# Attention with zero-padded k and v in SBUF, q stored unit by unit, transposes of 64 queries, and one MLP piece earlier

## The chip, the cores and the metric

The kernel runs on one core of one Trainium2 chip. The core has five engines that each work through their own instructions in order: TensorE (PE, with its weight loads shown apart as PEld), VectorE (DVE), ScalarE (ACT), GpSimd (POOL) and SyncE (SP), which here only issues DMA transfers. Engines wait for each other, and for transfers, through semaphores. The metric is the device time of one execution in microseconds (us); the kernel before takes 677.34 us, the median of three runs.

## The reference

Three layers follow each other. The first is attention with q, k, v of shape (2, 8, 576, 64): a pooled part and a local part, which are added.

```python
q_d = q.reshape(B, H, Sd, factor, D).mean(axis=3)      # factor = 4; k_d and v_d alike
out_d = sm_attn(q_d, k_d, v_d)                         # softmax attention over 144 pooled tokens
out_up = np.repeat(out_d, factor, axis=2)
mask = np.abs(pos[:, None] - pos[None, :]) < factor    # a query sees 3 keys on either side
scores = np.where(mask, scale * q @ k.T, -1e9)
...
return (out_up + softmax(scores) @ v).astype(np.float32)
```

Its output, 1152 tokens of 512 features, goes through `h = x @ w_in; g = h * clip(h + 3, 0, 6) / 6; g @ w_out` (hidden size 2048), and then through four weighted experts, `out += p[:, e] * (relu(x @ w1[e]) @ w2[e])` (hidden size 1024).

## The kernel before

**Units.** The attention works on eight units of two heads each, four for each of the two batches. For a unit, k and q stand with the 128 features of its two heads on the partitions and the 576 tokens along a row, and v stands with tokens on the partitions. Two units make a pair and share one k slot and one q slot; `load_qk` loads a pair (the first pair unit by unit), `load_v` loads a third of a batch's v.

**Local part.** The 576 queries are cut into 18 blocks of 32 (`WINDOWS`); a block sees 38 keys. `window(n)` gives the first of these keys, and at the two ends of the sequence it is moved inwards, so that the first and the last block have their queries elsewhere within their 38 keys than the other sixteen. The mask and the pooling weights `fours` therefore come in three kinds. `place(n)` sets a block's place: column group `j` (32 queries) and place `i`, whose parity `r = i % 2` says whether its keys stand on partitions 0 to 37 or 64 to 101 of a v slot. For this the v slots are loaded in runs of 112 rows (`WR2`: 48 rows from 0 on, and the next 64 from 64 on), which hold two blocks.

**Steps of a unit.** `sums` adds up k and q by fours on POOL (DVE for the first two units' k); `pooled_scores`, `masks`, `scores` are PE; `less_max`, `pooled_softmax`, `normalise`, `pooled_normalise` are DVE, ACT and POOL, where the last step is two POOL multiplications (`exd` by `recd`, `ex` by `rec`). `turn` transposes the 128 x 320 probabilities of each head on PE (`L610`) and copies them to `aT` on ACT; `pooled_turn` does so for the pooled part (`L678`). `values` multiplies by v (36 small products on `L698`, four pooled ones on `L709`) and adds both parts on DVE (`xf`).

**Order.** All engines follow the order in which the code is written during the attention. The loop over `t` interleaves the units: at turn `t` PE does `pooled_scores(t)`, `masks(t)`, `scores(t)`, `turn(t-1)`, `values(t-2)`, `pooled_turn(t-1)`; `idle_products` adds four 128 x 512 bf16 products of zeros ahead of `pooled_scores` and of `turn`, whose results are not used. POOL does the two multiplications of unit `t`, then `sums(t+2)`. SP issues transfers in the written order; up to eight are in flight, and the ninth waits for the first: pair 0, v of batch 0, pair 1, pair 2, the first weight block of the next layer (`w_in`), v of batch 1, and, written at the end of turn 1, pair 3. The last two turns (`t = 8, 9`) have no scores left; there `pieces(1)` puts single products of the next layer (`first`, 12 matrix products of 384 columns) between the steps. `convert` splits the next layer's weights into two parts on DVE and ACT, a step at a time.

Of the kernel before, what the change touches and what calls it, by code (L numbers as in the profile page):

```python
# [17 lines left out]
F32 = mybir.dt.float32  # L18
# [7 lines left out]
ALU = mybir.AluOpType  # L26
# [3 lines left out]
P = 128  # L30
# [9 lines left out]

QB = 32
# [8 lines left out]
WR2 = 112  # L50
# [8 lines left out]
NQ = 2 * QT + 2 * QB  # L59
# [53 lines left out]
def model(ctx: ExitStack, tc: tile.TileContext, qT, kT, v, dp, w_in, w_out, w1, w2, out):  # L113
# [246 lines left out]
    def load_qk(pair, units=(0, 1)):  # L360

        b, hp = divmod(2 * pair + units[0], NHP)
        if pair not in k_slots:
            k_slots[pair], q_slots[pair] = take(), take()
        n = len(units)
        at = units[0]
        nc.sync.dma_start(
            out=k_slots[pair][0][:, at * S : (at + n) * S].rearrange("p (u s) -> p u s", u=n),
            in_=kT[b, :, hp : hp + n],
        )  # L370
        q = q_slots[pair][0][:, : 2 * S].rearrange("p (s u c) -> p s u c", s=2, u=2)
        for s in range(2):
            nc.sync.dma_start(out=q[:, s, at : at + n], in_=qT[b, s, :, hp : hp + n, :])

    def window(n):
        return min(max(n * QB - (FACTOR - 1), 0), S - W)

# [10 lines left out]
    def load_v(b, p):  # L388
        v_slots.setdefault(b, []).append(take())
        if p < 2:  # L390
            if p == 0:
                v_rows(b, p, 0, window(0), WR, 0, 1)
                v_rows(b, p, WP, window(2), WR, 0, 1)
                v_rows(b, p, 0, window(1), WR2, 1, 2)
            else:
                v_rows(b, p, 0, window(8), WR2, 0, 2)
            v_rows(b, p, 0, window(8 * p + 4), WR2, 2, 4)
        else:
            v_rows(b, p, 0, window(16), WR, 0, 1)
            v_rows(b, p, 0, window(17), QB, 1, 2)  # L400
            v_rows(b, p, QB, window(17) + QB, W - QB, 1, 2)
# [8 lines left out]
    def pool_v(b):  # L410

        pool = banks(True)
        for m in range(4):
            for g in range(3):
                for r in range(2):
                    few = min(QB, KR[r] - g * QB)
                    if m * QB // FACTOR >= few:
                        continue
                    a, one = divmod(4 * g + m, 2)
                    n = 4 * a + 2 * r + one  # L420
                    i, j = place(n)
                    kind = 1 if n == 0 else 2 if n == NWIN - 1 else 0
                    rows = slice(r * WP, r * WP + W)
                    at = (3 - m) * QB // FACTOR
                    nc.tensor.matmul(
                        pool[g * QB : g * QB + few, r, :],
                        fours[rows, kind, at : at + few],
                        v_slots[b][i // 2][0][rows, j * DM : (j + 1) * DM],
                        start=(m == 0),
                        stop=((m + 1) * QB // FACTOR == few),  # L430
                    )
# [37 lines left out]
    def far(part, o):  # L469
        for sign in (1, -1):  # L470
# [4 lines left out]
                base=FACTOR - 1 + sign * o,  # L475
# [5 lines left out]
    far(mask[0:QB, 1:NI], FACTOR - 1)  # L481
    for j in range(1, NJ):
        nc.vector.tensor_copy(mask[j * QB : (j + 1) * QB, : NI - 1], mask[0:QB, 1:NI])
    far(mask[0:QB, 0:1], 0)
    far(mask[QB : 2 * QB, NI - 1 :], W - QB)
# [4 lines left out]
    fours = const.tile([P, 3, 7 * QB // FACTOR], F32, name="fours")  # L490

    def make_fours():
        nc.gpsimd.memset(fours[:WP], 0.0)
        own = slice(3 * QB // FACTOR, 4 * QB // FACTOR)
        nc.gpsimd.memset(fours[:WP, :, own], 1.0)
        for n, o in enumerate((FACTOR - 1, 0, W - QB)):
            for sign, at in ((1, -o), (-1, FACTOR - 1 + o)):
                nc.gpsimd.affine_select(
                    out=fours[:WP, n, own],
                    in_=fours[:WP, n, own],  # L500
                    pattern=[[-sign * FACTOR, QB // FACTOR]],
                    base=at,
                    channel_multiplier=sign,
                    compare_op=ALU.is_ge,
                    fill=0.0,
                )
# [6 lines left out]
    class Unit:  # L513
# [4 lines left out]
        def sums(self):  # L518
# [3 lines left out]
            self.k = k[:, o * S : (o + 1) * S]  # L522
            self.q = q[:, : 2 * S].rearrange("p (s u c) -> p s u c", s=2, u=2)[:, :, o]
            self.kd = k[:, 2 * S + o * PK : 2 * S + (o + 1) * PK]
            self.qd = q[:, 2 * S + o * PK : 2 * S + (o + 1) * PK]
            k4 = k[:, o * S : o * S + NI * QT]
            k4 = k4.rearrange("p (a r j f) -> p r a j f", a=NI, r=2, f=FACTOR)
            half = k[:, 2 * S + 2 * PK : 2 * S + 4 * PK].rearrange("p (j r) -> p j r", r=2)
            halves = k[:, 2 * S + 2 * PK :][:, : 4 * KR[0]]
            halves = halves.rearrange("p (a r j f) -> p r a j f", a=NI, r=2, f=2)  # L530
            if self.u >= 2:
                k2 = self.k.rearrange("p (j f) -> p j f", f=FACTOR)
                add(nc.gpsimd, half, k2[:, :, 0:2], k2[:, :, 2:4])
            for r in range(2):
# [3 lines left out]
                else:  # L538
                    two = halves[:, r, : NI - r]
                    add(nc.gpsimd, to, two[:, :, :, 0], two[:, :, :, 1])  # L540
            q4 = self.q.rearrange("p s (j r) -> p s j r", r=FACTOR)
            half = q[:, 2 * S + 2 * PK : 2 * S + 4 * PK]
            half = half.rearrange("p (s j r) -> p s j r", s=2, r=2)
            add(nc.gpsimd, half, q4[:, :, :, 0:2], q4[:, :, :, 2:4])
            qd = self.qd.rearrange("p (s j) -> p s j", s=2)
            add(nc.gpsimd, qd, half[:, :, :, 0], half[:, :, :, 1])
# [14 lines left out]
        def scores(self):  # L561
            for i, j, n in WINDOWS:
                q0, ks = n * QB, window(n)
                for h in range(2):
# [3 lines left out]
                        self.q[d, q0 // CH, q0 % CH : q0 % CH + QB],  # L568
                        self.k[d, ks : ks + W],
# [33 lines left out]
        def turn(self, idle):  # L603
# [3 lines left out]
            for h in range(2):  # L607
                for p in range(NP):
                    n = min(QT, NQ - p * QT)
                    nc.tensor.transpose(  # L610
                        tr[:, h, p * QT : p * QT + n],
                        self.ex[:n, h, 2 * p : 2 * p + 2, :].rearrange("q r w -> q (r w)"),
                        ident[:n, :n],
                    )
# [73 lines left out]
        def values(self):  # L688
# [3 lines left out]
            for i, j, _ in WINDOWS:  # L692
                p, r = divmod(i, 2)
                c0 = p * QT + j * QB
                keys = slice(r * WP, r * WP + W)
                for h in range(2):
                    at = j * DM + col[h]
                    nc.tensor.matmul(  # L698
                        pv[h * D : (h + 1) * D, r, c0 : c0 + QB],
                        v_slots[b][p][0][keys, at : at + D],  # L700
                        self.aT[keys, h, c0 : c0 + QB],
# [5 lines left out]
            for kc in range(2):  # L707
                for h in range(2):
                    nc.tensor.matmul(  # L709
                        pv[h * D : (h + 1) * D, 0, NQ : NQ + PK],  # L710
# [6 lines left out]
            nc.scalar.activation(out=pd[:, :PK], in_=pv[:, 0, NQ : NQ + PK], func=AF.Copy)  # L717
# [233 lines left out]
    for t in range(NU + 2):  # L951
# [248 lines left out]
```

## Time and profile before

| what | value |
|---|---|
| median of 3 runs | 677.34 us (676.77 to 677.75) |
| the profiled execution's own time | 674.32 us |
| its span from the first to the last instruction | 672.5 us |
| PE busy | 656.9 us, 98% of the span |
| DVE, ACT, POOL busy | 418.7, 251.7, 109.5 us |
| mean granted TensorE clock | 0.986 of full speed |
| attention, to the end of the last `values` | about the first 87 us |

The profile is of one execution, whose own time is the span and 1.8 us around it. It gives busy times by engine and line, what each engine waited for, and the chain of work that ended last. [...]

### The profile page before, as it was taken

How to read it: one execution, taken by the hardware profiler on the slowest of the kernel's cores; microseconds unless marked ns; L12 is line 12 of the kernel's file. 1: busy time of each engine (PE TensorE's matmuls, PEld its weight loads, DVE VectorE, ACT ScalarE, POOL GpSimd, SP SyncE). 2: the span in 40 equal slices, each digit the busy share in tenths (PEclk: the TensorE clock that was granted, in tenths of full speed). 3: DMA queues.
4: the chain of work that ended last, by engine and by line, in shares of the span. 5: the costliest groups of instructions: out<-in, count | busy, mean ns of one | idle time of the engine just before them, and what ended most of it. 6: DMA issues, size and time to landing. Idle time of an engine off the chain costs nothing.

```text
span 672.5 us, 11847 instructions
## 1 busy us (share of the span) xinstructions
PE 656.9 (98%) x4890; PEld 587.1 (87%) x4903; DVE 418.7 (62%) x815; ACT 251.7 (37%) x580; POOL 109.5 (16%) x148
## 2 busy tenths in 40 slices
PE   7899999999999999999999999999999999999997
PEld 3465899999998999989898898898998998988985
DVE  6376699952399328386575575575665665755642
ACT  3545575632365426354133142233233241331310
POOL 4654400000000016060120121201201201201000
PEclk8989799999999999999999999999999999999999
DMA  8943024400061011300030110110110110300012
GB/s 245 299 168 128 3 81 144 152 1 1 7 252 55 1 63 62 113 14 2 9 117 1 63 64 0 63 63 0 64 63 1 63 62 1 111 17 0 1 48 94
DMA packets 10462, 45.37 MB, mean 67 GB/s; under 512 B 1308, under 2 KB 1820, under 8 KB 6312
## 3 DMA queue, kind: packets, MB, share of 16 engines
q1 hardware_dynamic: 10408, 44.61, 19.9%
q8 instruction: 38, 0.62, 0.4%
q14 instruction: 16, 0.13, 0.1%
HBM read 42.25 MB, written 2.36 MB: 66 GB/s over the span
## 4 chain that ended last, share of the span: by engine, by line
PE 90%; DVE 6%; DMA 2%; issue 1%; POOL 0%; ACT 0%; SPq 0%; POOLq 0%
PE bank L856 25%; PE bank L1087 10%; PE bank L1086 10%; PE bank L1085 10%; PE bank L353 9%; PE bank L355 9%; PE bank L354 9%; PE pair L698 2%; PE pair L511 2%; PE pair L610 1%; DMA slot<-in_v_dram 1%; DVE slot L228 1%; PE pair L709 1%; DVE slot L207 1%; DVE slot L249 1%
## 5 line engine op out<-in xcount | busy, mean ns | idle before, releaser
L856 PEld LDWEIGHTS bank<-xop,slot 128*128 128x128 f32 x1344 | 180.3, 188 | 3.4 <-DVE u L404 2.0
L856 PE MATMUL bank<-xop,slot 128*128 128x288 f32 x1344 | 181.6, 295 | 1.6 <-DVE u L404 1.6
L1085 PE MATMUL bank<-slot,h 128*128 128x512 f32 x288 | 113.9, 396 | 0.0
L1086 PE MATMUL bank<-slot,h 128*128 128x512 f32 x288 | 113.9, 396 | 0.0
L1087 PE MATMUL bank<-slot,h 128*128 128x512 f32 x288 | 113.9, 395 | 0.0
L1093 DVE SCALAR_TENSOR_TENSOR slot<-bank,pr,slot 128x512 f32<-128x512 f32 x63 | 47.3, 751 | 85.9 <-PE bank L1087 85.9
L404 POOL TENSOR_TENSOR st<-slot 128x256 f32<-128x256 f32 x16 | 13.2, 828 | 441.2 <-DMA slot<-in_w_dram 206.3
L355 PE MATMUL bank<-h,slot 128*128 128x384 f32 x192 | 64.8, 337 | 1.2 <-DVE slot L207 1.2
L1087 PEld LDWEIGHTS bank<-slot,h 128*128 128x128 f32 x288 | 54.1, 188 | 13.1
L353 PE MATMUL bank<-x,slot 128*128 128x384 f32 x192 | 65.2, 340 | 0.0
L353 PE MATMUL bank<-h,slot 128*128 128x384 f32 x192 | 64.7, 337 | 0.5 <-ACT slot L202 0.5
L1085 PEld LDWEIGHTS bank<-slot,h 128*128 128x128 f32 x288 | 54.1, 188 | 12.3
L1086 PEld LDWEIGHTS bank<-slot,h 128*128 128x128 f32 x288 | 54.1, 188 | 12.3
L354 PE MATMUL bank<-x,slot 128*128 128x384 f32 x192 | 64.9, 338 | 0.0
L355 PE MATMUL bank<-x,slot 128*128 128x384 f32 x192 | 64.7, 337 | 0.0
L354 PE MATMUL bank<-h,slot 128*128 128x384 f32 x192 | 64.4, 336 | 0.0
L404 DVE TENSOR_TENSOR u<-bank,u 128x288 f32<-128x288 f32 x96 | 43.6, 454 | 20.9 <-PE bank L856 20.6
L885 ACT ACTIVATE h<-c 128x288 fp32r<-128x288 f32 x64 | 27.8, 445 | 72.8 <-DVE c L404 72.8
L771 DVE SCALAR_TENSOR_TENSOR slot<-t,bank 128x384 f32<-128x384 f32 x48 | 26.3, 552 | 32.5 <-ACT t L770 32.2
L770 ACT ACTIVATE t<-bank,half__169 128x384 f32<-128x384 f32 x48 | 27.7, 581 | 45.8 <-PE bank L355 45.8
L283 ACT ACTIVATE slot<-st 128x512 fp32r<-128x512 f32 x32 | 19.2, 624 | 63.3 <-POOL st L277 63.3
L779 DVE TENSOR_TENSOR h<-slot,h 128x384 fp32r<-128x384 f32 x48 | 27.8, 585 | 21.9 <-ACT h L778 21.9
(100 smaller groups left out, 943.2 us busy)
## 6 DMA issues: line engine op xcount, KB each, us to landing
slot<-in_w_dram SPq DMA_DIRECT2D x16, 1024.0 KB, 4.9
slot<-in_w_in_dram SPq DMA_DIRECT2D x8, 1024.0 KB, 5.3
slot<-in_w_out_dram SPq DMA_DIRECT2D x8, 1024.0 KB, 4.8
slot<-in_v_dram SPq DMA_DIRECT2D x6, 448.0 KB, 9.7
out_dram<-slot SPq DMA_DIRECT2D x9, 256.0 KB, 2.0
slot<-in_kT_dram SPq DMA_DIRECT2D x3, 576.0 KB, 8.4
slot<-in_qT_dram SPq DMA_DIRECT2D x6, 288.0 KB, 7.7
slot<-in_kT_dram SPq DMA_DIRECT2D x2, 288.0 KB, 3.6
```

Of the source, the lines that this page charges most:

```text
L353: nc.tensor.matmul(ps, wh, xh, start=first, stop=False)
L354: nc.tensor.matmul(ps, wh, xl, start=False, stop=False)
L355: nc.tensor.matmul(ps, wl, xh, start=False, stop=last)
L404: eng.tensor_tensor(out=out, in0=a, in1=b, op=ALU.add)
L770: nc.scalar.activation(out=t, in_=ps, func=AF.Relu, bias=half_, scale=1.0 / (6.0 * UP))
L779: nc.vector.tensor_tensor(out=g[:, 1, :], in0=u, in1=r32(g[:, 0, :]), op=ALU.subtract)
L856: nc.tensor.matmul(ps, a[:, i, k], b[:, j, k], start=start and k == 0 and n == 0, stop=stop and k == 1 and n == 2, skip_group_check=True,)
L885: nc.scalar.activation(out=self.h[:, 0, i, j], in_=of, func=AF.Relu)
L1085: nc.tensor.matmul(ps, hh, w[:, 0], start=(f == 0), stop=False)
L1086: nc.tensor.matmul(ps, hh, w[:, 1], start=False, stop=False)
L1087: nc.tensor.matmul(ps, hl, w[:, 0], start=False, stop=(f == NF - 1))
L1093: nc.vector.scalar_tensor_tensor(out=to, in0=ps, scalar=share, in1=to, op0=ALU.mult, op1=ALU.add)
```

## The change

k and v get zeros where a block would reach over an end of the sequence, so that all blocks are alike: `window` goes, the mask is one pattern with three columns struck out at each end, `fours` has one kind in place of three. A unit's k row grows from 576 to 582 tokens; its edges are set to zero by two POOL instructions after each `load_qk`, and the transfer of a pair writes two runs of 576 in place of one of 1152. v starts three rows earlier, and is loaded in runs of 128 rows (before, 112); the three and six rows beyond the ends are set to zero on DVE. q stands unit by unit in its slot, in runs of 288 (before, 576 for a pair). `turn` transposes 64 queries at a time, from partitions 0 to 63 into one PSUM bank and from 64 to 127 into the other, and copies `aT` with two ACT instructions. `values` takes its blocks in another order, with `r` changing fastest. In the loop the first piece of the next layer stands ahead of `values(6)` and no longer behind it.

```diff
-NQ = 2 * QT + 2 * QB
+HQ = 2 * QB
+SK = S + 2 * (FACTOR - 1)
...
     def load_qk(pair, units=(0, 1)):
...
-        nc.sync.dma_start(
-            out=k_slots[pair][0][:, at * S : (at + n) * S].rearrange("p (u s) -> p u s", u=n),
-            in_=kT[b, :, hp : hp + n],
-        )
-        q = q_slots[pair][0][:, : 2 * S].rearrange("p (s u c) -> p s u c", s=2, u=2)
+        k, q = k_slots[pair][0], q_slots[pair][0]
+        k = k[:, at * SK : (at + n) * SK].rearrange("p (u s) -> p u s", u=n)
+        nc.sync.dma_start(out=k[:, :, FACTOR - 1 : FACTOR - 1 + S], in_=kT[b, :, hp : hp + n])
+        for edge in (slice(0, FACTOR - 1), slice(SK - FACTOR + 1, SK)):
+            nc.gpsimd.memset(k[:, :, edge], 0.0)
+        q = q[:, at * S : (at + n) * S].rearrange("p (u s c) -> p s u c", u=n, s=2)
         for s in range(2):
-            nc.sync.dma_start(out=q[:, s, at : at + n], in_=qT[b, s, :, hp : hp + n, :])
+            nc.sync.dma_start(out=q[:, s], in_=qT[b, s, :, hp : hp + n, :])
...
     def load_v(b, p):
...
+        slot, o = v_slots[b][p][0], FACTOR - 1
+        if p == 0:
+            nc.vector.memset(slot[:o, :DM], 0.0)
+            v_rows(b, p, o, 0, WR, 0, 1)
+            v_rows(b, p, WP, WP - o, WP, 0, 1)
+            v_rows(b, p, 0, QB - o, P, 1, 2)
+            v_rows(b, p, 0, 4 * QB - o, P, 2, 4)
+        elif p == 1:
+            v_rows(b, p, 0, 8 * QB - o, P, 0, 2)
+            v_rows(b, p, 0, 12 * QB - o, P, 2, 4)
...
         def turn(self, idle):
...
-            for h in range(2):
-                for p in range(NP):
-                    n = min(QT, NQ - p * QT)
-                    nc.tensor.transpose(
-                        tr[:, h, p * QT : p * QT + n],
-                        self.ex[:n, h, 2 * p : 2 * p + 2, :].rearrange("q r w -> q (r w)"),
-                        ident[:n, :n],
-                    )
-            self.aT = att.tile([P, 2, NQ], F32, tag="aT", name="aT", bufs=2)
-            nc.scalar.activation(out=self.aT, in_=tr[:, :, :NQ], func=AF.Copy)
+            for p in range(NP):
+                for h in range(2):
+                    at = (2 * p + h) * HQ
+                    for b in range(2 if p < NP - 1 else 1):
+                        rows = slice(b * HQ, (b + 1) * HQ)
+                        nc.tensor.transpose(
+                            tr[:, b, at : at + HQ],
+                            self.ex[rows, h, 2 * p : 2 * p + 2, :].rearrange("q r w -> q (r w)"),
+                            ident[rows, rows],
+                        )
+            n = 2 * NP * HQ
+            self.aT = att.tile([P, n + n - 2 * HQ], F32, tag="aT", name="aT", bufs=2)
+            nc.scalar.activation(out=self.aT[:, :n], in_=tr[:, 0, :n], func=AF.Copy)
+            nc.scalar.activation(out=self.aT[:, n:], in_=tr[:, 1, : n - 2 * HQ], func=AF.Copy)
...
         def values(self):
...
-            for i, j, _ in WINDOWS:
-                p, r = divmod(i, 2)
+            for p, j, r in sorted((i // 2, j, i % 2) for i, j, _ in WINDOWS):
...
+        if t == NU:
+            pieces(1)
         if t >= NU:
             units[t - 2].values()
+        if t > NU:
             pieces(1)
-        if t > NU:
             units[t - 3].low(nc.gpsimd)
```

Three places show how the instructions stand now. The first is on POOL, around the two multiplications of unit 2 (`exd` and `ex_137`, in the changed kernel `ex_149`); the `slot` rows are `sums`, and DMAHW names the semaphore of a transfer. Before:

```order
L404 TENSOR_TENSOR slot<-slot 128x288
L404 TENSOR_TENSOR slot<-slot 128x144 [waits Pool_49]
L665 TENSOR_TENSOR exd<-exd,recd 72x576 [waits DVE_49,PE_49,Activation_49]
L599 TENSOR_TENSOR ex_137<-ex_137,rec 128x2x5x38 [waits DVE_49,Activation_49]
L404 TENSOR_TENSOR slot<-slot 128x288 [waits DMAHW2_49]
```

The same place on POOL in the changed kernel, where the two `MEMSET` rows are the edges of pair 3's k:

```order
L407 TENSOR_TENSOR slot<-slot 128x288
L407 TENSOR_TENSOR slot<-slot 128x144 [waits Pool_49]
L372 MEMSET slot 128x2x3 [waits DMAHW7_49,PE_49]
L372 MEMSET slot 128x2x3
L673 TENSOR_TENSOR exd<-exd,recd 72x576 [waits DVE_49,PE_49,Activation_49]
L602 TENSOR_TENSOR ex_149<-ex_149,rec 128x2x5x38 [waits DVE_49,Activation_49]
L407 TENSOR_TENSOR slot<-slot 128x288
```

The zeros of pair 3 stand between `sums(3)` and the multiplications of unit 2, and the first of them waits for a transfer on DMAHW7. The transfers take the eight semaphores in turn; the value waited for (64, four transfers of 16) is that of the fourth on DMAHW7, which is the load of pair 3's k itself: tracked as whole ranges, the padded row and its edges overlap.

The second place is on PE, from the pooled transposes of unit 6 (`exd`, L678, now L686) into turn 8. Before:

```order
L678 MATMUL pair<-ident,exd 80x72
L678 MATMUL pair<-ident,exd 64x72
L698 MATMUL pair<-aT,slot 64x32 x36
L709 MATMUL pair<-aTd,slot 64x144 x4
L353 MATMUL bank<-x,slot 128x384
```

The same place on PE in the changed kernel:

```order
L686 MATMUL pair<-ident,exd 80x72
L686 MATMUL pair<-ident,exd 64x72
L354 MATMUL bank<-x,slot 128x384
L355 MATMUL bank<-x,slot 128x384
L356 MATMUL bank<-x,slot 128x384
```

The piece (12 products, of which the first three stand here) now follows the pooled transposes at once. The third place is the local transposes of unit 7 on PE, a little later in turn 8, before:

```order
L610 MATMUL pair<-ident,ex_136 128x128 x2
L610 MATMUL pair<-ident,ex_136 128x64
L610 MATMUL pair<-ident,ex_136 128x128 x2
L610 MATMUL pair<-ident,ex_136 128x64
L678 MATMUL pair<-ident,exd 80x72
```

And in the changed kernel, on PE, from the values of unit 6 on:

```order
L706 MATMUL pair<-aT,slot 64x32 x36
L717 MATMUL pair<-aTd,slot 64x144 x4
L616 MATMUL pair<-ident,ex_148 128x64 x10
L686 MATMUL pair<-ident,exd 80x72
L686 MATMUL pair<-ident,exd 64x72
```

Six transposes of two widths have become ten of one width, in this turn and in the seven others, and they now come right behind the values of unit 6.

## Rows read from the trace of the kernel before

**Rows 1.** The page: busy time by engine, and TensorE's clock in 40 slices.

```profile
PE 656.9 (98%) x4890; PEld 587.1 (87%) x4903; DVE 418.7 (62%) x815; ACT 251.7 (37%) x580; POOL 109.5 (16%) x148
PEclk8989799999999999999999999999999999999999
```

**Rows 2.** Chain that ended last, 0 to 170 us: start, duration, what.

```profile
7.31 8.09 DMA slot<-in_v_dram
15.45 2.79 PE pair L425 x28
...
20.88 0.64 PE pair L624 x8
...
28.22 0.65 PE pair L624 x8
...
29.69 2.97 issue
...
34.96 1.41 PE pair L610 x6
...
40.08 0.65 PE pair L624 x8
...
42.73 0.99 PE pair L610 x6
43.72 1.42 PE pair L698 x72
45.14 0.79 PE pair L709 x8
...
73.82 2.41 PE pair L698 x72
76.23 1.35 PE pair L709 x8
```

**Rows 3.** Stretches: window, length, busy us (instructions) by engine, clock, DMA share, GB/s.

```profile
32.70:36.10 3.40, 3.18 (x33) 1.65 (x35) 2.64 (x7) 0.52 (x1) 0.55 (x1) 0.53 1.04 362
...
46.40:49.80 3.40, 3.18 (x17) 1.59 (x16) 2.94 (x8) 1.84 (x5) 2.25 (x5) 0.54 0.00 0
...
73.70:80.50 6.80, 6.80 (x91) 5.92 (x91) 2.79 (x6) 2.27 (x6) 3.72 (x4) 0.52 0.00 0
```

**Rows 4.** Weight loads on PE, 0 to 92 us: count, busy us, mean ns, idle before.

```profile
L698 PEld LDWEIGHTS pair<-aT,slot 38*64 38x64 f32 x576 | 12.0, 144 | 0.8 <-ACT slot L194 0.2 <-ACT pd L717 0.2
...
L610 PEld LDWEIGHTS pair<-ident,ex 128*128 128x128 f32 x32 | 4.0, 150 | 2.9 <-issue 1.3
...
L610 PEld LDWEIGHTS pair<-ident,ex 64*128 64x128 f32 x16 | 2.2, 139 | 2.9 <-issue 2.9
```

**Rows 5.** DMA in 8.7:12.7 (v), 15.6:22.2 (k, q, w_in) and 24:30 us (v).

```profile
DMA packets 564, 1.08 MB, mean 270 GB/s; under 512 B 36, under 2 KB 36, under 8 KB 564
...
DMA packets 852, 2.67 MB, mean 404 GB/s; under 512 B 94, under 2 KB 94, under 8 KB 757
...
DMA packets 758, 1.48 MB, mean 246 GB/s; under 512 B 56, under 2 KB 56, under 8 KB 753
```

**Rows 6.** The transfer of pair 3's k: issue, and time to landing.

```profile
L367 SPq DMA_DIRECT2D slot<-in_kT_dram x1: 346/346/346, 27.5 to 27.5; - x1
...
DMA to landing us min/median/max: 8.4/8.4/8.4
```

**Rows 7.** Timeline of POOL, 24 to 43 us: start, duration, what.

```profile
24.91 1.14 POOL L665 TENSOR_TENSOR exd<-exd,recd 72x576 f32<-72x576 f32 x1
26.02 0.82 POOL L599 TENSOR_TENSOR ex<-ex,rec 128x380 f32<-128x380 f32 x1
26.80 2.44 POOL L404 TENSOR_TENSOR slot<-slot 128x288 f32<-128x288 f32 x5
```

**Rows 8.** Timelines of DVE and PE around 85 us: start, duration, what.

```profile
85.29 1.29 DVE L207 TENSOR_TENSOR slot<-slot 128x512 fp32r<-128x512 f32 x2
...
87.03 0.44 PE L353 MATMUL bank<-x,slot 128*128 128x384 f32 x1
```

More of the change, by code (lines that the diff above doesn't have):

```diff
@@ L49 @@
 WR = 48
-WR2 = 112
+SK = S + 2 * (FACTOR - 1)
 def place(n):
@@ L389, in load_v @@
         v_slots.setdefault(b, []).append(take())
[L390 to L397, printed above, removed]
-        else:
-            v_rows(b, p, 0, window(16), WR, 0, 1)
-            v_rows(b, p, 0, window(17), QB, 1, 2)
-            v_rows(b, p, QB, window(17) + QB, W - QB, 1, 2)
+        slot, o = v_slots[b][p][0], FACTOR - 1
[8 more added lines that the diff above has]
+            v_rows(b, p, 0, 12 * QB - o, P, 2, 4)
+        else:
+            at = 16 * QB - o
+            nc.vector.memset(slot[QB:W, DM : 2 * DM], 0.0)
+            v_rows(b, p, 0, at, WR, 0, 1)
+            v_rows(b, p, 0, at + QB, QB, 1, 2)
+            v_rows(b, p, QB, at + 2 * QB, o, 1, 2)
     def add(eng, out, a, b):
@@ L426, in pool_v @@
                         pool[g * QB : g * QB + few, r, :],
-                        fours[rows, kind, at : at + few],
+                        fours[rows, at : at + few],
                         v_slots[b][i // 2][0][rows, j * DM : (j + 1) * DM],
@@ L467, in model, with far @@
     nc.gpsimd.memset(mask, 0.0)
-    def far(part, o):
+    def far(part):
         for sign in (1, -1):
@@ L474, in far @@
                 pattern=[[0, part.shape[1]], [-sign, W]],
-                base=FACTOR - 1 + sign * o,
+                base=(FACTOR - 1) * (1 + sign),
                 channel_multiplier=sign,
@@ L479, in far @@
             )
-    far(mask[0:QB, 1:NI], FACTOR - 1)
+    far(mask[0:QB])
     for j in range(1, NJ):
-        nc.vector.tensor_copy(mask[j * QB : (j + 1) * QB, : NI - 1], mask[0:QB, 1:NI])
-    far(mask[0:QB, 0:1], 0)
-    far(mask[QB : 2 * QB, NI - 1 :], W - QB)
+        n = NI if j < 2 else NI - 1
+        nc.vector.tensor_copy(mask[j * QB : (j + 1) * QB, :n], mask[0:QB, :n])
+    nc.vector.memset(mask[0:QB, 0, : FACTOR - 1], MASKED)
+    nc.vector.memset(mask[QB : 2 * QB, NI - 1, W - FACTOR + 1 :], MASKED)
     ident = const.tile([P, P], F32, name="ident")
@@ L489, in model @@
     nc.vector.memset(half_, 0.5)
-    fours = const.tile([P, 3, 7 * QB // FACTOR], F32, name="fours")
+    fours = const.tile([P, 7 * QB // FACTOR], F32, name="fours")
     def make_fours():
         nc.gpsimd.memset(fours[:WP], 0.0)
[L494 to L505, printed above, removed]
-                )
+        own = fours[:WP, 3 * QB // FACTOR : 4 * QB // FACTOR]
+        nc.gpsimd.memset(own, 1.0)
+        for sign, at in ((1, -(FACTOR - 1)), (-1, 2 * (FACTOR - 1))):
+            nc.gpsimd.affine_select(
+                out=own,
+                in_=own,
+                pattern=[[-sign * FACTOR, QB // FACTOR]],
+                base=at,
+                channel_multiplier=sign,
+                compare_op=ALU.is_ge,
+                fill=0.0,
+            )
         nc.gpsimd.tensor_copy(fours[WP:], fours[:WP])
@@ L538, in sums @@
                 else:
-                    two = halves[:, r, : NI - r]
+                    two = k2[:, r, : NI - r]
                     add(nc.gpsimd, to, two[:, :, :, 0], two[:, :, :, 1])
[L541 to L546, printed above, removed]
+            of = self.q.rearrange("p (j f) -> p j f", f=FACTOR)
+            half = q[:, room].rearrange("p (j f) -> p j f", f=2)
+            add(nc.gpsimd, half, of[:, :, 0:2], of[:, :, 2:4])
+            add(nc.gpsimd, self.qd, half[:, :, 0], half[:, :, 1])
         def masks(self, idle):
```

41 lines of the change are left out of this document (21 added, 20 removed).

## The prediction

> **What bounds the kernel now.** I read the page first, for the engine that has no time to spare. TensorE is busy for 656.9 us, and its clock shows less than 9 tenths only in the first, third and fifth of 40 slices; the other engines are far from full [rows 1]. So the time changes by what PE does or waits for, and since only the attention is edited, all of it must come from the first 87 us; behind them PE does the same work as before. I then followed the chain of waits through these 87 us. Three things in it are not PE at its full rate: v of batch 0, a transfer of 8.09 us that ends at 15.4 with PE waiting behind it; a stall of 2.97 us at 29.69 that the trace puts down to no engine; and steps that take longer than the same step elsewhere: `turn` 1.41 at 34.96 but 0.99 at 42.73, `values` 2.41 at 73.82 but 1.42 at 43.72, its pooled products 1.35 but 0.79 [rows 2]. [...] Last I read transfers, POOL and DVE for what PE will wait for once it runs sooner.
>
> The 0.2% by which a measurement here can tell two kernels apart is 1.35 us. The sum is made against the profiled execution's own 674.32 us; the median of the runs lies 3.02 above it, and I add that at the end.
>
> **1. v in 128 rows.** By the shapes, a batch's v grows from 1,932 to 2,182 KB (+13%), and each of its transfers reaches all partitions. v0 moved at 270 GB/s and v1 at 246, the 128-row transfers of k, q and `w_in` between them at 404 [rows 5]. The trace has no 128-row transfer with v's 2 KB runs. The two ends are 250 (the rate comes with v's layout in DRAM) and 404 (it comes with the rows); I take 390, near the row with the same number of partitions. Then v0 takes 5.7 in place of 7.6 us, 1.9 less, and lands at about 13.5.
>
> **2. A new wait on POOL.** Today POOL does `exd` and `ex` of unit 2 (1.14 and 0.82 us) at 24.91 and 26.02, long ahead of `turn(2)` [rows 7, 2]. In the changed order the zeros of pair 3's k stand ahead of the two, and they wait for that pair's k. Behind them are queued both multiplications, so `turn(2)` and `pooled_turn(2)` on PE. That k lands 8.4 us after its issue at 27.5, at 35.9 [rows 6]. This would be too late, so all hangs on how much sooner it lands. v0 gives 1.9. v1's bytes take 5.6 at 390 in place of 7.9 at 246, so 2.3. The k itself shares its 8.4 us with the tail of v1; at 404 GB/s the 2.67 MB of such a stretch took 6.6 [rows 5], so 1.8. It lands at 35.9 - 6.0 = 29.9, say **30.0**: between 28.8 (all 6.2 MB behind v0 at 404 GB/s: 13.5 + 15.3) and 31.7 (without the last 1.8). The shorter runs of q and the gap in k I cost at nothing to 0.3, within this.
>
> [...]
>
> `turn(2)` then starts at 30.0 + 0.1 (two memsets of 6 columns; POOL's five sums, of far more columns, take 0.49 each [rows 7]) + 1.14 + 0.82 = 32.1, before 34.96: 2.9 sooner. PE would have been there at about 28.6: pooled scores at 20.88 come 1.9 sooner, the next at 28.22 come 7.0 later (7.34 less item 3 and 4's savings), and `turn` starts 2.65 behind them as at 40.08 to 42.73 [rows 2]. So PE waits 3.5 us, and this wait hides whatever else the first 30 us gain or lose: q unit by unit, the edges in DVE and POOL of the first pairs, and the stall of 2.97, which if it stays would end PE's scores near 32.7, 0.6 later. After idling PE is likely to go on at the lower clock, as it does behind the stall at 29.69 [rows 2, 3]. Then `turn`, `values` and the pooled products take 0.42 (paid today too), 0.99 and 0.56 more, 1.55 that is new. With the savings of items 3 and 4 in this turn (0.34): 2.9 - 1.55 + 0.34 = **+1.7 us**.
>
> **3. Ten transposes of 64 queries in place of six.** On PE `turn` takes 0.99 us now [rows 2]. Its loads are the cost: 32 of 128 rows mean 150 ns and 16 of 64 rows mean 139 ns, and ahead of each of the latter PEld stands idle for 0.18 us (2.9 over 16), where both heights alternate [rows 4]. All loads of the new order have 64 rows of probabilities. If they follow one another, ten take 1.39, 0.4 more; six deep in each half of the array, 0.83, 0.16 less; if only the two changes of height a turn go (0.36), 0.63, 0.36 less. I take 0.74, so 0.25 less. Turns 3 to 7: **+1.25**.
>
> [...]
>
> **4. `values` with r fastest.** 72 products in 1.42 us, whose loads take 144 ns each [rows 2, 4]: 72 x 144 ns is 10.4 us, so some seven overlap already. Neighbours now differ in the half of the rows that they read. The bounds are nothing and eight at a time (1.30, 0.12 less); I take 0.09 each, nearer to eight, since the new neighbours share no rows: units 2 to 7 **+0.55**.
>
> **5. The low clock at 46.4.** 3.40 us at 0.54 lose 1.6 [rows 3]. PE reaches this stretch with other waits, and the trace cannot say if the clock falls there again. Half: **+0.8**, bounds 0 and 1.6.
>
> **6. The piece sooner.** 6.80 us from 73.7 at 0.52 lose 3.3 [rows 3]. They begin with `values(6)`, which follows `values(5)` and a pooled `turn` without wide products between, and cover a piece as well. In the changed order the piece stands between the two, and the longest run of narrow products is `values`, `turn` and pooled `turn`, as in the turn from 40.08 to 45.9, which had full speed [rows 2]. I take **+2.6**; bounds 0 (the low clock moves elsewhere) and 3.3.
>
> **7. DVE at the end.** The first product at 87.03 needs a conversion on DVE that runs from 85.29, two of 1.29 us in all [rows 8], so it has 0.5 us to spare. PE arrives sooner, DVE less so: **-0.3**, bounds 0 and -1.5.
>
> At nothing: the second copy on ACT, which is busy for 37% (`values` reads `aT` a whole turn of 7.3 us later; without that cover it would cost a turn no more than an operation like `ex` on POOL, 0.82), zeros of v on DVE, which waits for transfers then, and fewer steps for masks and `fours`.
>
> Sum: 1.7 + 1.25 + 0.55 + 0.8 + 2.6 - 0.3 = 6.6. 674.32 - 6.6 = 667.7, and with 3.02 **670.7 us**. Its own range, by the bounds of items 2 to 7 that don't all fall on one side, is 667.5 to 674. Chance 0.50.
>
> **Rivals.** *Slower: v still at 250 GB/s.* For it speaks that v0 and v1 had this rate at different times and beside different work [rows 5], against it the row count. v0 and v1 take 1.0 more each and pair 3's k 0.8 in its share, so it lands at 38.7 and `turn(2)` starts at 40.8: 5.85 later, 1.55 for the clock, 0.34 back, -7.1. Items 3 to 7 give 4.9, together -2.2: 679.5 us. It decides from a k that lands later than 36.6, 0.7 behind today's 35.9. Chance 0.16.
>
> *Faster: no low clock behind the wait.* k lands at 28.8, `turn(2)` starts at 30.9, 4.06 sooner and at full speed; with 0.34, items 3 and 4, all of 5 (1.6), 2.6 and -0.3 the sum is 10.1: 667.2 us. Against it: behind the stall at 29.69 the clock did fall. Chance 0.15.
>
> *Loads one after the other.* `turn` at 1.39: 0.65 worse than taken, in six turns 3.9: 674.6 us. Against it: loads of 64 rows overlap in `values`. Chance 0.06.
>
> *It gains nothing that can be told.* The low clock of 46.4 and 73.7 only moves (-3.4), and k lands at 31.7 (-1.7): 6.6 - 5.1 = 1.5, 675.8 us. For it: the clock's falls have no row that explains each. Chance 0.13, a quarter of it faster by over 0.2%.
>
> **Numbers.** Faster by over 0.2% (below 676.0): 0.50 + 0.15 + 0.06 + 0.03 = 0.74; within it 0.10; slower (above 678.7) 0.16. The range runs from 665.5 (beyond the fast rival, with its other terms at their bounds) to 678.0, short of the slow rival.
>
> **What would show it.** Pair 3's k landing near 30, GB/s near 390 in the stretches of v, a POOL memset that waits for that k, and PE's `turn(2)` waiting for POOL show items 1 and 2; a landing beyond 36.6 makes the prediction wrong in sign. Chain rows of the ten transposes (0.74) and 72 products (1.33) show 3 and 4, the granted clock behind `turn(2)`, near 46 and near 74 to 80 shows the last part of 2, 5 and 6, and the first product of the third piece waiting for DVE shows 7. Low clock in new places would take away what 5 and 6 give.

## The result and the profile after

| | kernel before | changed kernel |
|---|---|---|
| median of the runs | 677.26 us (676.77 to 677.75, 4 runs) | 669.88 us (667.77 to 673.15, 4 runs) |
| ratio, 95% interval | | 0.9895 (0.9854 to 0.9937) |
| the profiled execution's own time | 674.32 us | 667.77 us |

The kernel is 1.1% faster, and the total lies 0.8 us from the forecast of 670.7. The profile shows that it did not come about as forecast. First the page, for [rows 1]:

```profile
PE 648.6 (97%) x4922; PEld 583.1 (88%) x4935; DVE 424.3 (64%) x821; ACT 251.6 (38%) x588; POOL 109.9 (17%) x150
PEclk9799799999999999999999999999999999999999
```

PE is busy for 8.3 us less, and its mean granted clock is the same, 0.986. I then set the two timelines of PE side by side where the same work is done in both, ahead of `turn(6)` and at the third product of the third piece. Before:

```profile
69.71 1.16 PE L610 MATMUL pair<-ident,ex 128*128 128x128 f32 x6
87.49 0.34 PE L355 MATMUL bank<-x,slot 128*128 128x384 f32 x1
```

And the changed kernel (in brackets the idle time ahead and what ended it):

```profile
67.28 0.58 PE L616 MATMUL pair<-ident,ex 64*128 64x64 f32 x10
85.85 0.44 PE L356 MATMUL bank<-x,slot 128*128 128x384 f32 x1 [0.52 <-DVE slot L208]
```

At 67 us it leads by 2.4 us, at 86 us by 1.64. The spans differ by 6.7. So in this pair of executions 5.1 us come from behind the attention, where no line was edited. The groups by line find them. These are the longest groups of products before, in the last layer (count, busy us, mean ns, idle before):

```profile
L856 PE MATMUL bank<-xop,slot 128*128 128x288 f32 x1344 | 181.6, 295 | 1.6 <-DVE u L404 1.6
L1085 PE MATMUL bank<-slot,h 128*128 128x512 f32 x288 | 113.9, 396 | 0.0
```

The same two in the changed kernel:

```profile
L864 PE MATMUL bank<-xop,slot 128*128 128x288 f32 x1344 | 182.2, 295 | 1.5 <-DVE u L407 1.5
L1096 PE MATMUL bank<-slot,h 128*128 128x512 f32 x288 | 112.2, 390 | 0.0
```

The 512-column products take 390 ns in place of 396. There are three such groups of 288, PE is never idle ahead of them, and 864 x 6 ns is 5.2 us. Worked out from the starts of neighbours, one follows the other after 227.2 ns, before after 233.4. The instructions are the same. What differs is where their operands lie: the pooling weights `fours` have one kind in place of three, so every tile that is allocated behind them on the left side of SBUF lies 448 bytes lower (the first of the 8 KiB slots at 22,496, before at 22,944). `h`, on the right, has not moved.

In the attention, the chain of waits has the new steps on it, for [rows 2]:

```profile
18.02 6.32 DMA slot<-in_v_dram
...
36.45 0.58 PE pair L616 x10
37.04 1.28 PE pair L706 x72
...
40.60 0.65 PE pair L632 x8
...
43.26 0.52 PE pair L616 x10
43.78 1.28 PE pair L706 x72
...
72.08 0.42 DVE xf L731
72.64 0.66 PE bank L354
```

`turn` takes 0.52 us (0.99 before), `values` 1.28 (1.42). PE's timeline names the three waits of which the text below speaks:

```profile
16.45 5.35 PE L427 MATMUL pair<-slot,fours 38*16 38x512 f32 x28 [0.84 <-DMA slot<-in_v_dram]
...
36.45 0.58 PE L616 MATMUL pair<-ident,ex 64*128 64x64 f32 x10 [1.18 <-POOL ex L602]
...
72.64 0.66 PE L354 MATMUL bank<-x,slot 128*128 128x384 f32 x1 [1.29 <-DVE xf L731]
```

The windows, for [rows 3], show the lower clock in other places (length, busy us by engine, clock, DMA share, GB/s). In both traces the granted clock stands at 0.50 or at 1.00, and a window that holds both shows a value between; before, the long `turn` at 34.96 and the long `values` at 73.82 lie where it was 0.53 and 0.52 [rows 2, 3].

```profile
16.40:21.80 5.40, 5.35 (x30) 1.12 (x32) 1.08 (x3) 0.00 (x0) 3.30 (x8) 0.50 1.08 387
46.40:49.80 3.40, 3.35 (x97) 1.84 (x100) 3.37 (x8) 1.54 (x4) 3.11 (x5) 1.00 0.02 5
72.60:76.80 4.20, 4.16 (x16) 3.75 (x16) 0.86 (x1) 1.20 (x3) 1.74 (x2) 0.50 0.00 0
```

The transfers of v, in the stretches of [rows 5] (8.7 to 12.7 and 24 to 30 us), move 362 and 317 GB/s, before 270 and 246:

```profile
DMA packets 753, 1.45 MB, mean 362 GB/s; under 512 B 53, under 2 KB 53, under 8 KB 752
...
DMA packets 997, 1.90 MB, mean 317 GB/s; under 512 B 95, under 2 KB 95, under 8 KB 989
```

Pair 3's k is issued at 28.6 and lands 5.6 later, at 34.2 (the transfer's own row, as in [rows 6]):

```profile
L370 SPq DMA_DIRECT2D slot<-in_kT_dram x1: 385/385/385, 28.6 to 28.6; - x1
...
DMA to landing us min/median/max: 5.6/5.6/5.6
```

POOL's timeline shows the new wait, for [rows 7]:

```profile
34.31 0.14 POOL L372 MEMSET slot<- 128x6 f32 x2 [8.99 <-PE pair L569]
34.48 1.14 POOL L673 TENSOR_TENSOR exd<-exd,recd 72x576 f32<-72x576 f32 x1
35.58 0.82 POOL L602 TENSOR_TENSOR ex<-ex,rec 128x380 f32<-128x380 f32 x1
```

The row names PE's scores, which are written behind the zeros and cannot be what they wait for; they only ended at the same moment. The landing at 34.2 fits, and in a second profile of the changed kernel the same row names the transfer:

```profile
33.12 0.14 POOL L372 MEMSET slot<- 128x6 f32 x2 [9.10 <-DMA slot<-in_kT_dram]
```

### The profile page after: what moved, and what is told of

It reads as the page before. It is cut to its first block, busy times and chain, and to the rows that moved or that the text cites. A ratio compares the mean times of both kernels' runs of the same rounds, so it can differ in the third digit from the quotient of the medians.

```text
span 665.8 us, 11923 instructions
## 1 busy us (share of the span) xinstructions
PE 648.6 (97%) x4922; PEld 583.1 (88%) x4935; DVE 424.3 (64%) x821; ACT 251.6 (38%) x588; POOL 109.9 (17%) x150
## 4 chain that ended last, share of the span: by engine, by line
PE 85%; DVE 8%; DMA 3%; issue 1%; ACT 1%; POOL 1%; SPq 0%; DVEq 0%; ACTq 0%; POOLq 0%
PE bank L864 25%; PE bank L1096 10%; PE bank L1097 10%; PE bank L1095 10%; PE bank L356 9%; PE bank L354 9%; PE bank L355 9%; DVE slot L208 2%; DVE slot L250 1%; DMA slot<-in_kT_dram 1%; DVE slot L229 1%; PE pair L706 1%; DMA slot<-in_v_dram 1%; PE pair L513 1%; DMA slot<-in_qT_dram 1%
## 5 line engine op out<-in xcount | busy, mean ns | idle before, releaser
L864 PE MATMUL bank<-xop,slot 128*128 128x288 f32 x1344 | 182.2, 295 | 1.5 <-DVE u L407 1.5
L1096 PE MATMUL bank<-slot,h 128*128 128x512 f32 x288 | 112.2, 390 | 0.0
L1097 PE MATMUL bank<-slot,h 128*128 128x512 f32 x288 | 112.2, 390 | 0.0
L1095 PE MATMUL bank<-slot,h 128*128 128x512 f32 x288 | 112.1, 389 | 0.0
```

The lines of the kernel that those rows point to most:

```text
L864: nc.tensor.matmul(ps, a[:, i, k], b[:, j, k], start=start and k == 0 and n == 0, stop=stop and k == 1 and n == 2, skip_group_check=True,)
L1095: nc.tensor.matmul(ps, hh, w[:, 0], start=(f == 0), stop=False)
L1096: nc.tensor.matmul(ps, hh, w[:, 1], start=False, stop=False)
L1097: nc.tensor.matmul(ps, hl, w[:, 0], start=False, stop=(f == NF - 1))
```

## The experiments

Kernels that were run together share a chip, and each ratio is to runs of the kernel before on that chip.

| kernel | median us (runs) | ratio, 95% interval | 512-column product, ns |
|---|---|---|---|
| before, again | 678.38 (10) | 1.0005 (0.9973 to 1.0037) | 396 |
| before in the new place | 672.52 (7) | 0.9926 (0.9900 to 0.9952) | 390 |
| before, 64 bytes more | 672.85 (6) | 0.9910 (0.9877 to 0.9942) | 390 |
| changed, again | 669.26 (4) | 0.9878 (0.9843 to 0.9913) | 390 |
| changed in the old place | 676.46 (10) | 0.9979 (0.9951 to 1.0006) | 396 |
| changed, 32 bytes more | 672.60 (6) | 0.9927 (0.9903 to 0.9952) | 395 |
| changed, 128 bytes more | 675.29 (10) | 0.9943 (0.9914 to 0.9971) | 395 |
| v in 112 rows | 673.26 (4) | 0.9927 (0.9897 to 0.9956) | 390 |
| zeros of pair 3 first | 668.42 (4) | 0.9867 (0.9825 to 0.9909) | 390 |
| piece back | 670.31 (4) | 0.9879 (0.9845 to 0.9914) | 390 |
| old `turn` and `values` | 673.22 (10) | 0.9938 (0.9901 to 0.9976) | 390 |
| zeros first, waits filled | 668.11 (4) | 0.9834 (0.9788 to 0.9880) | 390 |

**The place in SBUF.** Four kernels: both as they are, and each in the other's place.

> The kernel before, unchanged. In the two profiles the first product of three in the last layer (512 columns, 864 of them) follows the one before it after 233.4 ns in the kernel before and after 227.2 ns in the changed one, which is 5 us of the 6.6 us between the two profiled executions. Theory P (where the tiles lie in SBUF: all tiles on the left side moved by 448 bytes, since the pooling weights have one kind in place of three) and theory R (something else in the changed program) expect 233 ns here again and a time within 0.3% of 677.3 us. Theory Q (chance from execution to execution, or the chip) expects that this can come out at 227 ns, and then about 672 us.

> The changed kernel, unchanged. P and R expect a spacing of 227 ns again, Q either value. Time 668 to 673 us by all three; by Q the slow ones of them have 233 ns. The attention alone (to the first products behind it) ends about 1.6 us sooner than in the kernel before by its profile, whatever the spacing.

The changed kernel with `fours` at its old size:

```diff
-    fours = const.tile([P, 7 * QB // FACTOR], F32, name="fours")
+    fours = const.tile([P, 3 * 7 * QB // FACTOR], F32, name="fours")[:, : 7 * QB // FACTOR]
```

> The changed kernel with the pooling weights' tile allocated at its old size (one third of it used), so that every tile on the left side of SBUF lies where it lay before, and no instruction differs. P expects a spacing of 233 ns and a time 4 to 5 us above the changed kernel (about 674 to 675 us); R expects 227 ns and the changed kernel's time; Q expects no relation to the edit.

And the kernel before with its slots at 22,496:

```diff
-    identb = const.tile([P, P], BF16, name="identb")
+    identb = att.tile([P, P], BF16, name="identb")
...
-    mask = const.tile([QT, NI, W], BF16, name="mask")
+    mask = att.tile([QT, NI, W], BF16, name="mask")
...
-    fours = const.tile([P, 3, 7 * QB // FACTOR], F32, name="fours")
+    n4 = 3 * 7 * QB // FACTOR
+    fours = const.tile([P, n4 + 48], F32, name="fours")[:, :n4].rearrange("p (k n) -> p k n", k=3)
```

This moves more than the slots: by the addresses of the built program, the two constants and the tiles `ex` on the right change their place, too.

> The kernel before with two small constants (identity in bf16 and mask) allocated on the right side and 192 bytes added to the pooling weights' tile, so that all the large tiles on the left lie where they lie in the changed kernel; the instructions are those of before. P expects a spacing of 227 ns and 4 to 5 us less than before (about 672 to 673 us); R expects 233 ns and 677 us; Q expects no relation to the edit.

The group of 512-column products in the changed kernel in the old place:

```profile
L1095 PE MATMUL bank<-slot,h 128*128 128x512 f32 x288 | 113.9, 396 | 0.0
```

And in the kernel before in the new place:

```profile
L1087 PE MATMUL bank<-slot,h 128*128 128x512 f32 x288 | 112.2, 390 | 0.0
```

The duration goes with the place in all four, whichever the code (theory P; worked out from the starts, 233.3 and 227.2 ns). In time, the new place is worth 677.44 - 672.52 = 4.9 us to the kernel before and 676.46 - 669.26 = 7.2 to the changed one. What is left for the edits themselves is 1.0 us in the old place (its interval holds zero) and 3.3 in the new.

Three more places ask how far the address matters. Two add to the tile of `fours` in the changed kernel, one in the kernel before:

```diff
-    fours = const.tile([P, 7 * QB // FACTOR], F32, name="fours")
+    fours = const.tile([P, 7 * QB // FACTOR + 8], F32, name="fours")[:, : 7 * QB // FACTOR]
```

> The changed kernel with 32 bytes added to a small tile, so that every large tile on the left of SBUF lies 32 bytes higher and the 8 KiB slots start at multiples of 1 KiB (22,528 in place of 22,496). [...]

The same with `+ 32`:

> The changed kernel with 128 bytes added to a small tile, so that the slots start at 22,624. Where they start at 22,496 the 512-column products follow one another after 227.2 ns, at 22,944 and 22,528 after 233.3. If the place counts within 128 bytes (the three lie 96, 32 and 0 bytes behind a multiple of 128, and the weights of these products, h, 96 too), 22,624 with its 96 gives 227 again and about 669.3 us; if a longer stretch counts, it gives 233 and about 673.

And the kernel before with `n4 + 16` columns in the tile, no other edit:

> The kernel before with 64 bytes added to a small tile, nothing else: its slots start at 23,008. So far 22,944, 22,528 and 22,624 gave 232 to 233 ns between the 512-column products, 22,496 gave 227.2. 23,008 agrees with 22,496 in its distance from a multiple of 512 bytes (480) but not of 1,024. If the place counts within 512 bytes, this gives 227 ns and about 672.5 us, as the kernel before in the changed kernel's place did; if it counts over a longer stretch (22,496 and h lie 992 bytes behind a multiple of 1,024), it gives 233 and about 677.5 us.

22,528 (233.2 ns) and 22,624 (232.3) keep the long spacing, 23,008 (227.2) has the short one. So 32 bytes decide, a start at a multiple of 1 KiB is no help, and 64 bytes added to a constant gave the kernel before nearly 1%. 22,496 and 23,008 agree in their distance from a multiple of 512 bytes, 480; the other three lie at 416, 0 and 96. They agree in that from a multiple of 256, too (224; the other three 160, 0 and 96), so the period stays open.

The changed kernel with 32 bytes more has the spacing of the kernel before and is still 5.3 us faster than it (672.60 against 677.92 on its chip, interval clear of zero), the one with 128 bytes more 2.7 us, of which 1 us belongs to its 232.3 ns. So at like spacing the edits themselves gain 1.0, 1.7, 3.3 and 5.3 us by the medians: a gain, but not one of 6.6.

The nine profiles of these kernels, whose attention is either that of before or that of the changed kernel, tell the two effects apart. From PE's timeline: when its last wait for v of batch 0 ends, when `turn(2)` and `turn(6)` start and the granted clock between the two, when the third product of the third piece starts, and the time from there to the end of the span (us):

| profile | slots at | v0 | `turn(2)` | `turn(6)` | clock | third piece | to the end |
|---|---|---|---|---|---|---|---|
| before | 22,944 | 15.45 | 34.76 | 69.71 | 0.93 | 87.49 | 585.0 |
| before, again | 22,944 | 16.55 | 38.80 | 77.34 | 0.83 | 95.31 | 585.1 |
| before in the new place | 22,496 | 16.21 | 35.41 | 72.69 | 0.86 | 90.45 | 579.9 |
| before, 64 bytes more | 23,008 | 15.96 | 35.82 | 73.17 | 0.86 | 90.98 | 579.8 |
| changed | 22,496 | 16.45 | 36.45 | 67.28 | 1.00 | 85.85 | 579.9 |
| changed, again | 22,496 | 15.11 | 35.84 | 69.56 | 0.90 | 87.31 | 581.4 |
| changed in the old place | 22,944 | 14.96 | 35.18 | 65.99 | 1.00 | 84.60 | 586.7 |
| changed, 32 bytes more | 22,528 | 14.55 | 34.80 | 65.61 | 1.00 | 84.34 | 584.9 |
| changed, 128 bytes more | 22,624 | 14.83 | 35.09 | 67.29 | 0.95 | 85.17 | 585.2 |

Behind the attention the place alone counts, 579.9 us against 585.0 with either code. (The two longer ones, 581.4 and 586.7, have a stretch at a granted clock of 0.83 from 295 to 305 us, the others 1.00.) Ahead of it the changed code leads, by 0.2 to 11.0 us as one pairs the profiles; the 1.64 above is one such pair, near its lower end. The lead arises from `turn(2)` to `turn(6)`, 35.0 to 38.5 us before and 30.8 to 33.7 in the changed code.

**v in 112 rows.**

```diff
-            v_rows(b, p, 0, QB - o, P, 1, 2)
-            v_rows(b, p, 0, 4 * QB - o, P, 2, 4)
+            v_rows(b, p, 0, QB - o, WP + WR, 1, 2)
+            v_rows(b, p, 0, 4 * QB - o, WP + WR, 2, 4)
```

and so for the other third.

> The changed kernel with the 128-row transfers of v cut back to 112 rows (the rows left out are read by nobody). If the rate comes with the rows, v goes back to 250 to 270 GB/s (128 rows: 310 to 390 in the profile of the changed kernel), and although 12% less is moved, pair 3's k lands about as late as in the kernel before (36 us; changed kernel 33.0 and 34.2); turn 2, which waits for it through POOL, starts 2 us later and the time is about 1.5 to 2.5 us more, 671 us. Rival: the rate comes with v's layout in DRAM, the transfers stay where they were or gain by the fewer bytes: 668.5 to 669.5 us.

The same stretches of its transfers:

```profile
DMA packets 582, 1.13 MB, mean 284 GB/s; under 512 B 35, under 2 KB 35, under 8 KB 581
...
DMA packets 806, 1.54 MB, mean 257 GB/s; under 512 B 63, under 2 KB 63, under 8 KB 803
```

The rate comes with the rows, 284 and 257 GB/s in place of 362 and 317, and the time is 0.5% more than the changed kernel's (0.9927 against 0.9878), 3.3 us, though the intervals overlap a little. With 7/8 of the rows the rate is 284/362 and 257/317 of what it was, about 0.8; what makes it so is not shown.

How the time comes about is not shown. The zeros of pair 3, which wait for its k, start at 35.12 on POOL (32.65 to 34.31 in the five profiles of the changed code above), but PE then waits for POOL only 0.48 us, since it has stood still for 1.16 itself; `turn(2)` starts at 37.27, not 2 us later but 0.8 to 2.5.

**Zeros of pair 3 ahead of its load.**

```diff
+        if pair < 3:
+            nc.sync.dma_start(out=k[:, :, FACTOR - 1 : FACTOR - 1 + S], in_=kT[b, :, hp : hp + n])
         for edge in (slice(0, FACTOR - 1), slice(SK - FACTOR + 1, SK)):
             nc.gpsimd.memset(k[:, :, edge], 0.0)
+        if pair == 3:
+            nc.sync.dma_start(out=k[:, :, FACTOR - 1 : FACTOR - 1 + S], in_=kT[b, :, hp : hp + n])
```

> The changed kernel with the zeros of pair 3's k written ahead of its load (the slot is free by then), so that POOL's multiplications of unit 2 are no longer queued behind the landing. If that wait lies on the path, turn 2 no longer waits the 1.2 us for POOL that the profile of the changed kernel shows, and the time is 1 to 1.5 us below its 669.3 us (668). Rival: another wait or the low clock takes its place, and the time stays within 0.5 us.

PE's waits in 10 to 95 us no longer name POOL:

```profile
PE pair L430 <- DMA slot<-in_v_dram: 2.7, 2, 1.4
PE bank L354 <- DVE xf L734: 1.6, 1, 1.6
PE pair L572 <- issue: 0.5, 1, 0.5
```

The ratio, 0.9867 against 0.9878, points the right way and lies within the intervals; the wait is gone, its price stays unsettled.

**The piece behind `values(6)` again** (the order of the kernel before).

```diff
-        if t == NU:
-            pieces(1)
         if t >= NU:
             units[t - 2].values()
+            pieces(1)
         if t > NU:
-            pieces(1)
             units[t - 3].low(nc.gpsimd)
```

> The changed kernel with the first piece of the next layer behind the values of unit 6 again. By the prediction's item 6 the piece's place is worth 2.6 us, so this would take 672 us, with a stretch at the lower clock from the values of unit 6 on. Rival: the low clock only moves, and in the new place the piece waits for VectorE's x (1.3 us in the profile of the changed kernel), so the place is worth nothing or loses: 668 to 669.5 us.

The ratio is that of the changed kernel, 0.9879 against 0.9878, and the low clock is there again, only later (windows, columns as above):

```profile
68.00:78.00 10.00, 8.93 (x263) 6.62 (x264) 8.13 (x15) 5.33 (x18) 5.58 (x6) 0.86 0.02 3
78.00:84.00 6.00, 6.00 (x37) 5.30 (x38) 1.65 (x4) 2.42 (x6) 1.74 (x2) 0.66 0.01 3
```

The medians differ by 1.0 us and the intervals allow some 3 either way; the forecast 2.6 do not show, but the time alone does not exclude them.

**The old `turn` and `values`.** Six transposes, one copy to `aT`, and `for i, j, _ in WINDOWS` with `self.aT[keys, h, c0 : c0 + QB]`, as before.

> The changed kernel with the six transposes of two heights, one copy to aT and the old order of the products of values, as in the kernel before; everything else stays, the place in SBUF too. By the rows, turn goes back from 0.52 to 0.99 us and values from 1.28 to 1.42, 0.6 a unit, 4.9 us over eight. Theory A: all of it lies on the path, 674 us. Theory B: PE waits for VectorE's x ahead of the first piece anyway (1.3 to 1.6 us in the profiles of the changed kernel), so that this wait swallows its share and 3.4 us are left, 672.7 us. Theory C: the prediction's sizes (0.25 and 0.09), 2.5 us, 671.8 us.

In its chain both steps are back at the old length:

```profile
46.50 0.99 PE pair L614 x6
47.49 1.42 PE pair L702 x72
```

0.6% more than the changed kernel, 4.0 us, lie between theories A (4.9) and B (3.4), which this doesn't tell apart. C is refuted by the rows, 0.61 us a unit where I had 0.34, not by the time, whose interval holds it.

**The waits for v filled.** The zeros of pair 3 first, and in `pool_v(0)`:

```diff
+                if tr is not None and m == 0 and g:
+                    idle_products(tr, FILL[g - 1])
```

with `FILL = (10, 5)` and `tr` the bank pair that `turn(0)` uses next.

> The changed kernel with the zeros of pair 3's k ahead of its load, and with 10 and 5 products of zeros (128 x 512, bf16, as the kernel has them elsewhere) in the two places in which PE waits for v of batch 0 between the pooled products of v (2.4 and 0.8 us in the profile of the changed kernel), behind which it ran at the lower clock in most profiles (the 28 products behind took 5.35 us there, and 2.79 in the kernel before). If the waiting brings the lower clock there, the 28 products take about 2.8 us, turn 2 starts 3 to 5 us sooner and the time is about 3 us below 668.4 (665.5). Rival: the low clock comes anyway or later, or the products of zeros delay what v would have released: 667.5 to 669.5 us.

Its timeline of PE:

```profile
16.10 2.79 PE L433 MATMUL pair<-slot,fours 38*16 38x512 f32 x28
...
31.44 1.23 PE L712 MATMUL pair<-aT,slot 38*64 38x32 f32 x66
35.04 0.36 PE L712 MATMUL pair<-aT,slot 38*64 38x32 f32 x6 [2.37 <-issue]
```

The 28 products take 2.79 us (granted clock 1.00 from 16 to 22 us) and `turn(2)` starts at 30.9, 5.5 us sooner. Then PE stands still in the midst of `values(1)` for 2.37 us that no semaphore explains, and goes on at the lower clock (windows):

```profile
22.00:32.00 10.00, 9.44 (x305) 6.31 (x281) 6.29 (x16) 7.49 (x27) 6.89 (x17) 1.00 1.05 317
34.00:44.00 10.00, 8.96 (x146) 5.20 (x145) 4.71 (x14) 3.87 (x14) 2.61 (x6) 0.66 0.45 180
```

`turn(3)` starts at 43.15, in the changed kernel at 43.19: the whole lead is given back (one profile of each). It is the fastest kernel by its ratio, 0.9834 against 0.9878, but the intervals don't tell the two apart.

## Why the prediction was right in the total and wrong in its steps

**What bounds the kernel.** The step that failed is the sentence "behind them PE does the same work as before". It does the same instructions, but 864 of them are 6 ns shorter, 5.2 us that I had put at nothing because no row of before could show them. The sum of 6.6 for the attention came to 1.64 in the two profiles, and to between 1.0 and 5.3 by the times at like spacing; that the total of 6.55 agrees is chance. Two premises were weak as well. The sum starts from one profile, in which the lower clock took less of the attention than in the three others of the same code (granted clock 0.91 from 0 to 92 us, there 0.83, 0.89 and 0.87; in all five profiles of the changed code 0.91). And 0.2% is less than these runs can tell: single executions of the unchanged kernel took from 674.06 to 682.94 us, and the intervals are 0.3 to 0.5% to either side.

**1. v.** Right that the rate comes with the rows; 362 and 317 GB/s, not 390. In the first profile PE's wait for v0 ends at 16.45, 1.0 later than in [rows 2], but in the other four of the changed code at 14.55 to 15.11, against 15.45 to 16.55 in the four of before: 0.9 sooner on average, with 13% more to move, where I had 1.9. (The 7.6 us for today's v0 were too long: 1,932 KB at the 270 GB/s of [rows 5] take 7.2.)

**2. The wait on POOL.** The mechanism was there, in all five profiles of the changed code (1.1 to 2.8 us); the size was wrong. k landed at 34.2, not 30.0, sooner than today's 35.9 but not by enough: `turn(2)` starts at 36.45, forecast 32.1, before 34.96 [rows 2]; over the profiles of the table it starts 0.7 sooner on average, where I had 2.9. The low clock behind the wait came in two of the five (granted clock 0.57 from 36 to 44 us in the second profile). In all five it came 20 us earlier, in the 28 pooled products behind the wait for v0 (4.1 to 5.4 us; before, 2.79 in three of four profiles). The stall of 2.97 is one of 2.0 to 3.5 us in all four profiles of the code before, and in the changed code one of 0.44 in one of five. By the pooled scores of turn 4, at 40.60 in place of 40.08, the term is -0.5 in the first pair, where I had +1.7; over the nine profiles they start 3.6 sooner on average, so that one pair cannot size it.

**3 and 4. `turn` and `values`.** Right, and too small: 0.47 and 0.14 a unit, forecast 0.25 and 0.09. The ten loads do overlap (140 ns each by the median at 43.19, all ten in 0.45 us), and the rival in which they follow one another is out. From `turn(2)` to `turn(6)` that is 4 x 0.61 = 2.4 of the 5.4 us that the changed code gains on average there; the rest goes with the clock (0.83 to 0.93 before, 0.90 to 1.00 after). By the idle time at the two changes of height a turn [rows 4], `turn` would have gained 0.36; the trace gives more.

**5. The low clock at 46.4.** The granted clock is 1.00 there now, so 1.6 where I had 0.8; together with items 3 and 4 the lead grows from -0.5 to +2.4 us at `turn(6)`. But where it falls is no property of the edit: another execution of the kernel before has it elsewhere, too (0.63 from 16 to 22 us, where the first has 1.00 from 15.45 to 29.69).

**6 and 7. The end.** Item 6 failed. The low clock moved to the piece itself, which now waits for VectorE's x (`xf`, 1.29 us; 1.3 to 1.6 in all five profiles) and runs at 0.50 from 72.6 to 76.8. Item 7, a wait of 0.52 for DVE, came about as forecast (0.3). From `turn(6)` to the third piece the changed kernel loses 0.8 us (0.5 on average over the nine profiles), though `turn` and `values` are shorter there as well.

Of the rivals, the slower one had the right reason in a weaker form (k late), and the one that "gains nothing that can be told" fits the changed kernel in the old place (0.9979, with one within its interval), but not with 32 bytes more, at the same spacing (0.9927, 0.9903 to 0.9952).

## What to carry to other kernels

A tile that shrinks moves everything behind it: before an effect is put down to the code that was edited, run the old code at the new addresses, and the new code at the old ones. Where all the time lies in a few kinds of products, try some paddings of a small constant first; it is the cheapest edit there is, and here 64 bytes took 5.9 us off the kernel before (678.70 on its chip, 672.85), the edits themselves 1.0 to 5.3. And price a stretch from several profiles of the same kernel: one pair gave 1.64 us for the attention, others from 0.2 to 11. And a lead gained ahead of a stretch that waits for transfers is worth nothing until one has seen what the faster engine waits for there: the 5.5 us gained at `turn(2)` with the waits filled were gone by `turn(3)`.

## What the runs showed of the hardware

Products of 512 columns follow one another after 227 or 233 ns by the start address of the tiles on the left, at five addresses, with 32 bytes enough to tell. The 1344 products of 288 columns show no such gain (295 ns at both; their group is 0.6 us longer in the new place, 182.2 against 181.6). Which of the operands minds, and why, stays open: the slots moved against `h`, and `h` itself was not moved.

In ten of the 14 profiles PE stands still where no semaphore explains it, in eleven stalls of 0.4 to 3.5 us; 29.7 to 32.7 us in the kernel before [rows 2] and 32.7 to 35.0 in the one with the waits filled are two of them. In these two stretches the packets of queue q1 take 102.1% and 105.4% of the time of the 16 DMA engines, and one transfer on the instruction queue of 16 KB is in flight:

```profile
q8 instruction: 1, 0.02, 2.6%
```

(29.6 to 32.7 us of the kernel before; the share is 2.4% in the other stretch.) Such a transfer alone says little, for 38 of them stand in the first profile, most without a stall. But the stalls come at two places in PE's order whatever the kernel: ten before about the 948th of its loads and products, in the scores of unit 3 (with 25 of their products left where `turn` has six transposes, 33 where it has ten, and 48 where 15 products of zeros more stand ahead as well), and one 257 further on. And in all eleven PE goes on 1.3 to 1.7 us after the last such transfer has ended (31.00 and 32.66 in the kernel before, 33.56 and 35.04 with the waits filled). In the four profiles without a stall it reaches the first place 1.4 to 2.7 us after one. That PE waits for its own instructions would fit all of this, but no run shows it.

The lower clock falls at different places in two executions of one kernel: in the first profile of the kernel before at 32.7, 46.4 and 73.7 us, at 0.52 to 0.54 [rows 3]. In the second profile of the kernel before it lies here:

```profile
16.00:22.00 6.00, 5.45 (x32) 1.59 (x33) 0.95 (x3) 1.22 (x3) 3.56 (x7) 0.63 1.05 406
44.00:51.00 7.00, 7.00 (x107) 3.99 (x103) 3.83 (x8) 3.05 (x13) 0.42 (x1) 0.69 0.00 1
84.00:90.00 6.00, 6.00 (x24) 4.83 (x23) 1.52 (x4) 1.57 (x4) 1.68 (x2) 0.56 0.00 0
```

That execution's span is 680.4 us, 7.9 more than the first, 7.8 of it by the attention. A forecast that counts such a stretch as lost or won, as items 5 and 6 did, counts one throw.
